# Moving the scans of two units and the last weight conversions in an RWKV-7 and feed-forward kernel

## The chip, the cores and the metric

The kernel runs on one core of a Trainium2 chip. The metric is the device time of one execution in microseconds; for each version several runs are taken and the median is compared. One further execution was recorded by the hardware profiler.

## The reference

The first half is an RWKV-7 recurrence over 768 steps for 4 batches of 8 heads of 40 features, all in float32. Its output is laid out as 3072 tokens of 320 features and goes through a feed-forward block with a hard-swish.

```python
for t in range(S):
    y[:, :, t] = np.einsum('bhd,bhde->bhe', rt, state)
    Sa = np.einsum('bhde,bhe->bhd', state, at)
    state_decay = state * wt[:, :, None, :] - np.einsum('bhd,bhe->bhde', Sa, bt)
    state = state_decay + np.einsum('bhd,bhe->bhde', vt, kt)
...
x = attn_out.transpose(0, 2, 1, 3).reshape(B * S, H * D)
h = x @ w_in                                   # 320 -> 2048
g = h * np.clip(h + 3.0, 0.0, 6.0) / 6.0
return g @ w_out                               # 2048 -> 320
```

## The kernel before

Time is cut into blocks of 64 steps. A unit is one block of two batches with all 8 heads, so 128 partitions; there are 24 units, in groups of four (NU = 4). Units 0 to 3 are group 0, and this document is about them and about the preparation of units 4 to 7.

Each unit is prepared and then stepped. Preparation (`prepare`, line 534) has named stages. W transposes the decays on TensorE (PE), copies them into a work tile `wm` and runs a scan for the running products (L555). gam takes a reciprocal, runs a second scan (L566) and copies the results into `gam` and `rgam`, two copies on VectorE (L579) and two on GpSimd (L583, L584), with `dec` (L586). A and B transpose a and b and multiply them by the gammas (L599, L607); K does so for k (L687); F, factor, E and EV make the block's triangular matrix, the scaled rows KBt, and products with them. A whole group's F is inverted by a long chain of small VectorE operations (`invert`, L733 to L767), and products of the blocks (`third_block`, L788 and L811, called X and Y for group 0) finish the inverse `tinv`.

Stepping (`step`, line 832) has the stages RT, VT (transposes), R (L868, L872), S, U and UT (products with `tinv`), C and H (masked scores, L522 and L530), rS, sn (the state's sum, L961 and L969), y (L984; L995 on VectorE, then L996 `yg` on GpSimd), and `move`, `move2`, which copy yg by eight DMAs into `xt`, the feed-forward's input. Units 0 and 1 start from a zero state. Two yg buffers are shared by `ys` and `yg`.

The feed-forward of a unit is two jobs (unit, half). A job's `expand` is five pieces of matmuls into the PSUM tile h (L1066) and, at its end, L1081 on ScalarE and L1082 on VectorE; its `contract` is four pieces (L1107). `pieces(n)` issues n pieces between other work, job after job in the order of `jobs`; when the next job may not start, nothing is issued. A job may start when the unit's `move2` was issued and enough weights are converted.

The two weight matrices come in 20 pieces of raw data that are converted on the chip: three ScalarE operations each (`power`, L384 to L386) and three on VectorE (L369, L372, L360). The generator `load_weights` yields after each of these steps, so one piece is four steps; `deal(n)` takes n steps.

All instructions are issued in a hand-made order, and each engine runs its own in that order. For group 0 this order is the text PLAN (line 1282): a line is one t, an entry such as `2rS:3` runs stage rS of unit 2 and deals three weight steps right behind the PE work of that stage, ahead of the copies out of PSUM that follow it. P and Q are units 4 and 5 with the stages W and gam only, one stage for each mention. At t = 8 `seconds()` takes over a tile that held raw weights; from t = 8 on pieces are issued behind each line, and from t = 10 on each line is followed by one turn of `by_twos`, which prepares units 4 to 7 in twos (A of 4 and 5 at t = 12; W of 6, B of 4, W of 7, B of 5 at t = 13; K at 14, factor at 15, then F). At t = 10 A of 5 and W of 7 are fetched, at t = 11 B and K of 5, at t = 12 V of 4 and 5 and R of 4. What weight steps are left when the PLAN ends follows in one go.

All DMAs wait in one queue on SyncE (SP in the profile), in order of issue; a DMA whose condition is not met holds up those behind it. Inside W of a unit the next decays for the same buffer are fetched: W of 4 issues the DMAs of W of 6.

PSUM banks: transposes take turns between the single bank "one" and the two-deep "pair"; the other products use "pair".

Of the kernel before, what the change touches and what calls it, by code (L numbers as in the profile page):

```python
# [17 lines left out]
P = 128  # L18
# [13 lines left out]
def kernel(  # L32
# [47 lines left out]
    NU = 2 * NP  # L80
# [141 lines left out]
    for i in range(3):  # L222
        t = const.tile([P, H, BL], F32, name=f"score{i}")
# [14 lines left out]
    for p in range(NP):  # L238
        t = const.tile([P, 2, NPR, SLOT], F32, name=f"state{p}")
        nc.vector.memset(t[:], 0.0)  # L240
        state.append(t)
        t = const.tile([P, 2, NPR], F32, name=f"last{p}")
# [16 lines left out]
    for i, (x, y) in enumerate([(0, DFF // 2), (0, NJ // 2)]):  # L259
        for n, z in enumerate((x, y)):  # L260
            t = win[:, :, z:z + H * SLOT] if i == 0 else \
                wout[:, z:z + 4, :].rearrange("p j m -> p (j m)")[:, 0:2 * H * SLOT].rearrange(
                    "p (n x) -> p n x", n=2)
            t = t.rearrange("p n (h e) -> p n h e", e=SLOT)
# [4 lines left out]
    for u in range(2):  # L269
        t = win2[:, u * NPR * P:(u + 1) * NPR * P]  # L270
        placed["rgam", 2 + u] = t.rearrange("p (r t) -> p r t", t=P)
    WC = 256
    PIECES = 20
    converted = [0]
# [163 lines left out]
    NK = NG * NU  # L438
# [3 lines left out]
    def fetch(name, i, engine=None):  # L442

        if i is None or i >= NK:
            return
        x, crossed = {"W": (w, 0), "A": (a, 0), "B": (b, 0), "K": (k, 0), "R": (r, 1),
                      "V": (v, 1)}[name]
        if name == "V":
            t = values[i % AHEAD]
        else:  # L450
            t = placed.get((name, i))
            if (name, i) == ("R", 1):
                t = others["K"]
            if (name, i) == ("W", NU + 1):
                t = values[NU]
            t = t if t is not None else (others if i < 2 * NU and i % 2 and name != "R" else inputs)[name]
        g, p = names[i]
        engines = engine or nc.sync
        for q in range(2):
            engine = engines[q] if isinstance(engines, tuple) else engines  # L460
            y = x[2 * p + q, :, g * BL:(g + 1) * BL, :]
            rows = slice(q * BL, (q + 1) * BL)
            if crossed:
                for s in range(2):
                    engine.dma_start(out=t[rows, 4 * s:4 * s + 4, 0:D],
                                     in_=y[s::2].rearrange("h t e -> t h e"))
            else:
                engine.dma_start(out=t[rows, :, 0:D], in_=y.rearrange("h t e -> t h e"))  # L468
        data[i][name + "N"] = t

    def following(i):

        if i < 2:
            return None
        if i < 2 * NU:

            return i + 2 if i % NU < NU - 2 or i % 2 == 0 else None
        return i + 1

    def turn_pairs(x):  # L480

        o = ps_any([P, NPR, P])
        for n in range(NPR):
            nc.tensor.transpose(out=o[:, n, :],  # L484
                                in_=x[:, 2 * n:2 * n + 2, :].rearrange("p s e -> p (s e)"),
                                identity=ident[:])
        return o
# [46 lines left out]
    def prepare(i, F):  # L534
        n, o = i % NU, data[i]
        halves = i >= 2 * NU
        def w_stage():
            wt = turn_pairs(o["WN"])
            yield PE

            wm = o["wm"] = wms[i % 2]
            wv = wm[:, 0:SCAN].rearrange("p (r m i) -> p r m i", m=2, i=HB + 1)
            x = wt[:].rearrange("p r (q m i) -> p (r q) m i", q=2, m=2)
            if i in (0, NU, NU + 1):
                nc.vector.tensor_copy(wv[:, :, 0, 1:HB + 1], x[:, :, 0, ::-1])
            else:
                nc.scalar.activation(out=wv[:, :, 0, 1:HB + 1], in_=x[:, :, 0, ::-1], func=AF.Copy)
            if i in (0, NU, NU + 1):
                nc.vector.tensor_copy(wv[:, :, 1, 1:HB + 1], x[:, :, 1, :])
            else:  # L550
                nc.scalar.activation(out=wv[:, :, 1, 1:HB + 1], in_=x[:, :, 1, :], func=AF.Copy)  # L551
            if i != NU + 1:
                fetch("W", following(i))
            prods = o["prods"] = tmp.tile([P, NB, 2, HB + 1], F32, name="prods", bufs=2)
            nc.vector.tensor_tensor_scan(  # L555
                out=prods[:].rearrange("p r m i -> p (r m i)"), data0=wm[:, 0:SCAN], data1=start[:],
                initial=0.0, op0=ALU.mult, op1=ALU.add,
            )
# [154 lines left out]
    def in_turn(stages, order):  # L713

        for name in order:
            yield from stages[name]()
            shared[0] = None
            yield DONE

    def by_stages(i, stages):  # L720


        scanned = [] if i < NU + 2 else ["W", "gam"]
        order = ["K", "factor", "F"] if i % NU < 2 else ["K", "F", "factor"]
        return in_turn(stages, scanned + ["A", "B"] + order + ["E", "EV"])
# [299 lines left out]
    HJ, NQ = NJ // 2, 4  # L1025
    SPLIT = 2
    ready = {}
    jobs = deque([(i, r) for r in range(2) for i in range(SPLIT)])
    jobs.extend((i, r) for i in range(SPLIT, NK) for r in range(2))
    sums = {}  # L1030
    narrow, spread, LATEST = [], [False], 2

    def available():
        if not jobs:
            return False
        i, r = jobs[0]
        return i in ready and converted[0] >= (PIECES // 2 if i < SPLIT and r == 0 else PIECES)

    def feed_forward():

        last = None
        while True:
            while not available():
                if last:
                    yield from contract(*last)
                    last = None
                yield None
            i, r = jobs.popleft()
            gts = []
            yield from expand(ready[i], r * NQ, gts)  # L1050
            if last:
                for n, x in enumerate(contract(*last)):
                    if n == LATEST and narrow:
                        narrow[0]()
                    yield x
            if narrow:
                narrow[0]()
            last = (i, r, gts)
# [82 lines left out]
    def pieces(n):  # L1141

        owed[0] += n * (8 / 9 if spread[0] else 1)
        while owed[0] >= 1:
            owed[0] -= 1
            if not next(stream):
                owed[0] = 0.0

    def aside(n, weight=0):

        for _ in range(n):
            if side and next(side[0], side) is side:
                side.popleft()
            due[0] += weight
            while due[0] >= 1:
                due[0] -= 1
                next(weights, None)

    def deal(n):

        for _ in range(n):
            next(weights, None)

    def run(stage, steps=0, mixed=0, deals=0):

        for at in stage:
            if at == DONE:
                return
            aside(steps, mixed)
            deal(deals)  # L1170
# [13 lines left out]
    def prepared(i):  # L1184
        nonlocal F
        if i >= NK:
            return None
        if i % NU == 0:
            F = lazy_F()
        return prepare(i, F)  # L1190
# [6 lines left out]
    def by_twos(first, steps, mixed, rate):  # L1197


        chains = [by_stages(first + i, prepared(first + i)) for i in range(NU)]  # L1200
        for t in range(TWOS):

            order = [0, 1] if t < STAGES else []
            order += [2, 3] if t > 5 else []
            if t < 2:
                order = [0, 1, 0, 1][4 * t:]
            if t == 3:
                order = [2, 0, 3, 1]
            for i in order:
                if t >= 2 or first != NU:  # L1210
                    run(chains[i], steps if t > 10 else 0, mixed)
                pieces(rate / 2)
            if t == 10:
                side.append(invert(group_F[-1], third, first == 0))
            yield
# [12 lines left out]
    chains = [in_turn(begin[i], [x[1:] for x in FIRST + BESIDE if x[0] == str(i)]) for i in range(NU)]  # L1228
# [17 lines left out]
    chains = [in_turn(stages[0], ["RT", "VT", "C", "R"]), in_turn(stages[1], ["RT", "VT", "C"])]  # L1246
# [25 lines left out]
    def block(i, j):  # L1272

        if i % NU < 2:
            if j == 0:
# [4 lines left out]


    PLAN = """X X:2 0U:4 0UT:2 1R
              0sn:2 0H:1 Y:2 P
              1U 1UT:2 0y P
              2RT:1 Y:1 Q
              1sn:1 1H:1 2VT:2 0move 0move2
              1y:2 2R Q
              2S:3 3RT:2
              1move 1move2 2U:3 2UT:1 2C:5
              3R:4 3VT  # L1290
              2rS:3 2sn:3 2H:4 3S:2
              2y:3 3U:1 3UT:10 3C:5
              3rS:1 3sn:2 3H:4 2move
              3y:1 2move2

              3move
              3move2"""
# [2 lines left out]
    chains = {str(i): in_turn(stages[i], [x[0][1:] for line in plan for x in line if x[0][0] == str(i)])  # L1300
              for i in range(NU)}
# [187 lines left out]
```

## Time and profile before

| what | value |
|---|---|
| time, median of 3 runs | 792.41 us (791.11 to 794.02) |
| profiled execution, time | 788.99 us |
| its span, first to last instruction | 787.3 us |
| granted TensorE clock, mean | 0.972 |
| PE busy | 723.7 us (92%) |
| VectorE (DVE) busy | 496.1 us (63%) |
| ScalarE (ACT) busy | 320.0 us (41%) |
| GpSimd (POOL) busy | 175.0 us (22%) |

A line of the timeline has start and duration in us, engine, source line, operation, tiles written and read, shape, count, and in brackets the idle time of that engine before it with what ended it. A line of the busy time by stretch has the stretch, its length, then busy us and instructions for each engine, the granted clock, and the DMA engines' share and rate. "x4" at SPq means four DMAs issued; the time is that of their issue, and they land later. PEld, the weight load of a matmul, runs beside PE.

### The profile page before, as it was taken

What the parts mean: (1) busy time and instruction counts of PE and PEld (TensorE: products, weight loads), DVE (VectorE), ACT (ScalarE), POOL (GpSimd) and SP (SyncE); (2) the same over time, 40 slices, a digit from 0 to 9 for tenths busy, and PEclk for the clock granted to TensorE, in tenths of its full rate; (3) what the DMA queues carried; (4) which work ended last, traced back from release to release, by engine and by line L of the source; (5) the groups of instructions that cost most, each with busy time, mean ns of one, the idle gap of its engine ahead of it and who ended that gap; (6) DMA issues with size and microseconds to landing.
All of it is one profiled execution on the core that took longest, in us unless ns stands there. A gap on an engine that the chain in (4) does not pass through costs nothing.

```text
span 787.3 us, 35307 instructions
## 1 busy us (share of the span) xinstructions
PE 723.7 (92%) x15832; PEld 614.3 (78%) x15832; DVE 496.1 (63%) x971; ACT 320.0 (41%) x664; POOL 175.0 (22%) x318
## 2 busy tenths in 40 slices
PE   4626679999999989999999999999999999999998
PEld 3625668778778878888888888888888888888886
DVE  7899995598545699345888445987435982323210
ACT  2377982214445324444334534335534224412211
POOL 6403113122222304112404212304312201000000
PEclk9856999999999999999999999999999999999999
DMA  9684554411332313223213223213221101110000
GB/s 123 115 194 129 127 153 69 75 26 29 55 68 54 66 25 58 51 43 66 46 30 64 45 48 62 50 28 64 45 55 34 33 8 30 30 30 10 14 19 17
DMA packets 174215, 45.03 MB, mean 57 GB/s; under 512 B 157424, under 2 KB 172784, under 8 KB 174064
## 3 DMA queue, kind: packets, MB, share of 16 engines
q1 hardware_dynamic: 169760, 42.03, 27.8%
q8 instruction: 125, 2.05, 1.1%
q10 hardware_dynamic: 4304, 0.74, 0.7%
q14 instruction: 26, 0.21, 0.1%
HBM read 34.08 MB, written 3.93 MB: 48 GB/s over the span
## 4 chain that ended last, share of the span: by engine, by line
PE 77%; DVE 8%; issue 5%; SPq 4%; DMA 3%; ACT 2%; POOL 1%; DVEq 0%; POOLq 0%; ACTq 0%
PE h L1066 27%; PE o L1107 24%; PE pair L522 4%; PE pair L984 3%; PE pair L494 2%; PE pair L961 2%; PE one L484 2%; SPq L468 2%; PE pair L906 2%; PE pair L868 2%; DVE prod L753 1%; DVE x L759 1%; PE pair L926 1%; PE pair L942 1%; PE pair L701 1%
## 5 line engine op out<-in xcount | busy, mean ns | idle before, releaser
L1066 PE MATMUL h<-xt,win 128*128 128x128 f32 (+1 forms) x2304 | 249.2, 282 | 2.8 <-DVE gt L1082 2.0
L1066 PEld LDWEIGHTS h<-xt,win 128*128 128x128 f32 (+1 forms) x2304 | 229.9, 191 | 19.8 <-issue 5.0
L1107 PE MATMUL o<-wout,gt 128*128 128x320 f32 x768 | 230.4, 443 | 0.0
L1107 PEld LDWEIGHTS o<-wout,gt 128*128 128x128 f32 x768 | 138.4, 190 | 50.3 <-issue 0.2
L1082 DVE SCALAR_TENSOR_TENSOR gt<-gt,h 128x512 f32<-128x512 f32 x96 | 62.0, 681 | 71.4 <-ACT gt L1081 71.3
L1081 ACT ACTIVATE gt<-h,three 128x512 f32<-128x512 f32 x96 | 62.1, 685 | 101.9 <-PE h L1066 101.4
L996 POOL TENSOR_TENSOR yg<-ys,gam 128x512 f32<-128x512 f32 x22 | 39.0, 1774 | 156.3 <-DVE ys L995 83.6
L753 DVE TENSOR_TENSOR prod<-x 128x30 f32<-128x30 f32 (+9 forms) x180 | 67.2, 373 | 8.8 <-POOL x L738 3.3
L674 POOL TENSOR_TENSOR KBt<-K,rgt 128x320 f32<-128x320 f32 x22 | 19.0, 866 | 215.6 <-ACT rgt L663 177.8
L759 DVE TENSOR_TENSOR x<-x,prod 128x30 f32<-128x30 f32 (+9 forms) x180 | 62.2, 346 | 5.5
L969 DVE TENSOR_TENSOR state<-pair,state 40x320 f32<-40x320 f32 (+1 forms) x43 | 20.9, 487 | 60.8 <-PE pair L961 34.5
L530 DVE COPY_PREDICATED score<-mask,pair 128x512 f32<-128x512 int32 x72 | 50.6, 723 | 0.5
L995 DVE TENSOR_TENSOR ys<-pair,ys 128x512 f32<-128x512 f32 x22 | 15.2, 691 | 42.9 <-PE pair L701 21.8
L566 DVE TENSOR_TENSOR_SCAN wm<-wm,start 128x528 f32<-128x528 f32 x24 | 37.5, 1562 | 0.8
L555 DVE TENSOR_TENSOR_SCAN prods<-wm,start 128x528 f32<-128x528 f32 x24 | 30.1, 1259 | 10.4 <-ACT wm L551 10.3
L846 ACT ACTIVATE RT<-pair 128x512 f32<-128x512 f32 x22 | 13.1, 596 | 52.8 <-PE pair L494 52.8
L706 ACT ACTIVATE EV<-pair 64x320 f32<-64x320 f32 x44 | 19.0, 431 | 33.7 <-PE pair L701 23.0
L821 ACT ACTIVATE tinv<-pair 32x256 f32<-32x256 f32 x48 | 17.9, 374 | 31.7 <-PE pair L811 31.1
L1125 ACT ACTIVATE ob<-o 128x320 f32<-128x320 f32 x22 | 9.6, 435 | 49.4 <-PE o L1107 29.6
L583 POOL COPY gam<-prods 128x256 f32<-128x256 f32 x24 | 22.0, 916 | 30.7 <-DVE prods L555 26.9
L872 DVE TENSOR_TENSOR RR<-pair,EV 128x320 f32<-128x320 f32 x22 | 10.7, 487 | 25.4 <-PE pair L522 25.4
L984 PE MATMUL pair<-score,KBt 64*64 64x64 f32 x1408 | 25.9, 221 | 0.5 <-issue 0.5
(272 smaller groups left out, 1066.1 us busy)
## 6 DMA issues: line engine op xcount, KB each, us to landing
V<-in_v_dram SPq DMA_DIRECT2D x96, 40.0 KB
out_dram<-ob SPq DMA_DIRECT2D x47, 80.0 KB
R<-in_r_dram SPq DMA_DIRECT2D x92, 40.0 KB
B<-in_b_dram SPq DMA_DIRECT2D x42, 80.0 KB
K<-in_k_dram SPq DMA_DIRECT2D x42, 80.0 KB
W<-in_w_dram SPq DMA_DIRECT2D x37, 80.0 KB
A<-in_a_dram SPq DMA_DIRECT2D x37, 80.0 KB
xt<-yg SPq DMA_DIRECT2D x72, 40.0 KB
```

The source lines that it names most:

```text
L522: nc.tensor.matmul(out=o[i][half(q), n, :], lhsT=lhs[half(i, D), n ^ (2 * q * swap), half(q)], rhs=rhs[half(i, D), n, half(q)], start=True ...
L530: nc.vector.copy_predicated(out=x[:].rearrange("p (i h) t -> p i h t", i=2), mask=mask8, data=o[2])
L555: nc.vector.tensor_tensor_scan(out=prods[:].rearrange("p r m i -> p (r m i)"), data0=wm[:, 0:SCAN], data1=start[:], initial=0.0, op0=ALU.m ...
L566: nc.vector.tensor_tensor_scan(out=back, data0=back, data1=start[:], initial=0.0, op0=ALU.mult, op1=ALU.add)
L753: nc.vector.tensor_tensor(out=pv, in0=_ap(x[:], (i + 1) * L + i, [[L, n], [0, i]]), in1=_ap(x[:], i * L, [[0, n], [1, i]]), op=ALU.mult,)
L759: nc.vector.tensor_tensor(out=rest, in0=rest, in1=pv, op=ALU.add)
L984: nc.tensor.matmul(out=y[q][half(s), pr, :], lhsT=o[name][half(q), h * D:h * D + SLOT], rhs=m[name][half(q), 4 * rs + 2 * s + j, :], start ...
L996: nc.gpsimd.tensor_tensor(out=yg[:], in0=m["ys"][:].rearrange("p r q t -> p r (q t)"), in1=o["G"][:], op=ALU.mult)
L1066: nc.tensor.matmul(out=hp[c][:, i, :], lhsT=lhsT, rhs=rhs, start=(begun[c] == 0), stop=(begun[c] == 3 * NQ - 1))
L1081: nc.scalar.activation(out=gt[:], in_=hp[c][:], func=AF.Relu, bias=three[:], scale=1.0)
L1082: nc.vector.scalar_tensor_tensor(out=gt[:], in0=gt[:], scalar=6.0, in1=hp[c][:], op0=ALU.min, op1=ALU.mult)
L1107: nc.tensor.matmul(out=op[:], lhsT=gts[c][:, n, :], rhs=wout[:, c * HJ + r * NQ + n, :], start=((split or r == 0) and c == 0 and n == 0), ...
```

## The change

Four things, all in the stretch of group 0 and the preparation of units 4 and 5:

- the stages W and gam of units 4 and 5 (P, Q in the PLAN) are issued at t = 11, behind H of unit 3, and at t = 12, behind y of unit 3; before, they stood between t = 1 and t = 5;
- their copies into `wm` run on ScalarE, as those of other units do;
- the first half of unit 2 becomes the third job of the feed-forward, followed by its second half and the second halves of units 0 and 1, and it may start with half of the weights converted;
- from t = 7 on fewer weight steps are dealt, and the rest at t = 12 and within `by_twos` (one step for each PE stage while its own count is under 5).

```diff
-            if i in (0, NU, NU + 1):
+            if i == 0:
                 nc.vector.tensor_copy(wv[:, :, 0, 1:HB + 1], x[:, :, 0, ::-1])
             else:
                 nc.scalar.activation(out=wv[:, :, 0, 1:HB + 1], in_=x[:, :, 0, ::-1], func=AF.Copy)
-            if i in (0, NU, NU + 1):
+            if i == 0:
                 nc.vector.tensor_copy(wv[:, :, 1, 1:HB + 1], x[:, :, 1, :])
...
-    jobs = deque([(i, r) for r in range(2) for i in range(SPLIT)])
-    jobs.extend((i, r) for i in range(SPLIT, NK) for r in range(2))
+    jobs = deque([(0, 0), (1, 0), (2, 0), (2, 1), (0, 1), (1, 1)])
+    jobs.extend((i, r) for i in range(SPLIT + 1, NK) for r in range(2))
...
-        return i in ready and converted[0] >= (PIECES // 2 if i < SPLIT and r == 0 else PIECES)
+        return i in ready and converted[0] >= (PIECES // 2 if i <= SPLIT and r == 0 else PIECES)
...
-                    run(chains[i], steps if t > 10 else 0, mixed)
+                    run(chains[i], steps if t > 10 else 0, mixed, 1 if t < 5 else 0)
...
     PLAN = """X X:2 0U:4 0UT:2 1R
-              0sn:2 0H:1 Y:2 P
-              1U 1UT:2 0y P
-              2RT:1 Y:1 Q
+              0sn:2 0H:1 Y:2
+              1U 1UT:2 0y
+              2RT:1 Y:1
               1sn:1 1H:1 2VT:2 0move 0move2
-              1y:2 2R Q
+              1y:2 2R
               2S:3 3RT:2
-              1move 1move2 2U:3 2UT:1 2C:5
-              3R:4 3VT
-              2rS:3 2sn:3 2H:4 3S:2
-              2y:3 3U:1 3UT:10 3C:5
-              3rS:1 3sn:2 3H:4 2move
-              3y:1 2move2
+              1move 1move2 2U:2 2UT:1 2C:3
+              3R:2 3VT
+              2rS:1 2sn:2 2H:2 3S:2
+              2y:2 3U:1 3UT:1 3C:4
+              3rS:1 3sn:2 3H:4 P Q 2move
+              3y:3 P Q 2move2
```

## The prediction

> **What bounds the kernel now.** The page came first: PE is busy for 723.7 of 787.3 us, and its busy tenths are low only in the first seven slices. After 200 us PE is idle 11.0 us of 587, so its work there is fixed and a delay handed to it reaches the end whole. Then busy time by stretch, cut where the change acts: from unit 1's first product to unit 3's R (74.3 to 93.6), to the end of unit 3's H (119.2), to F of unit 4 (134.0), to the B transposes of unit 6 (147.5).
>
> ```profile
> core 0: us, PE busy (x) PEld busy (x) DVE busy (x) ACT busy (x) POOL busy (x), PEclk, DMA share, GB/s
> 74.30:93.60 19.30, 12.35 (x510) 10.46 (x505) 18.57 (x38) 18.30 (x33) 4.23 (x11) 1.00 0.62 144
> 93.60:119.20 25.60, 20.93 (x553) 19.16 (x553) 23.45 (x40) 21.59 (x33) 3.05 (x6) 0.93 0.50 137
> 119.20:134.00 14.80, 14.80 (x176) 12.80 (x180) 7.68 (x13) 2.63 (x7) 2.28 (x4) 1.00 0.37 62
> 134.00:147.50 13.50, 11.62 (x298) 9.18 (x297) 8.01 (x18) 4.46 (x9) 6.25 (x10) 1.00 0.41 76
> ```
>
> Two things are to be seen. In the first stretch VectorE and ScalarE are both full, not VectorE alone. In the third PE is full while VectorE has 7.1 us free: the change moves VectorE work out of the first two and into the third.
>
> The timeline of VectorE gives the price of one early scan and gamma (unit 4):
>
> ```profile
> 75.53 0.42 DVE L545 COPY wm<-one 128x256 f32<-128x256 f32 x1
> 75.86 0.41 DVE L549 COPY wm<-one 128x256 f32<-128x256 f32 x1
> 76.31 1.26 DVE L555 TENSOR_TENSOR_SCAN prods<-wm,start 128x528 f32<-128x528 f32 x1
> ...
> 78.89 0.25 DVE L564 RECIPROCAL start<-prods 128x16 f32<-128x16 f32 x1
> 79.17 1.26 DVE L566 TENSOR_TENSOR_SCAN wm<-wm,start 128x528 f32<-128x528 f32 x1
> ```
>
> With L579 and L568 behind it, 2.0 us for the scan and 2.0 us for the gamma, so 8.1 us for both units. One weight piece (L369, L372, L360) is 0.42 + 0.69 + 0.69 = 1.8 us of VectorE, and its three L384 to L386 are 2.2 us of ScalarE.
>
> The timeline of SyncE's queue, in which every DMA waits its turn:
>
> ```profile
> 80.75 1.28 SPq L468 DMA_DIRECT2D W<-in_w_dram  x2
> ...
> 112.62 3.10 SPq L1010 DMA_DIRECT2D xt<-yg  x4
> 116.80 2.02 SPq L468 DMA_DIRECT2D B<-in_b_dram  x2
> 118.93 1.28 SPq L468 DMA_DIRECT2D K<-in_k_dram  x2
> 120.25 3.41 SPq L1015 DMA_DIRECT2D xt<-yg  x4
> 123.71 5.30 SPq L465 DMA_DIRECT2D V<-in_v_dram  x8
> ```
>
> From 120.25 on the queue has no gap until 153.9: `2move2`, V, R, A, A, W, `3move`, `3move2`, then unit 6's B at 142.51. PE and GpSimd feel that queue once each, in the timeline:
>
> ```profile
> 125.06 1.27 POOL L996 TENSOR_TENSOR yg<-ys,gam 128x512 f32<-128x512 f32 x1 [5.92 <-DMA xt<-yg]
> 133.95 1.59 PE L621 MATMUL pair<-bt,at 40*32 40x64 f32 x128
> 147.50 0.63 PE L484 MATMUL one<-ident,B 128*128 128x128 f32 x4 [1.88 <-DMA B<-in_b_dram]
> ```
>
> Unit 3's yg on GpSimd cannot start before unit 2's `2move2` has landed (two yg buffers), and PE loses 1.88 us for B.
>
> **Part 1, what leaves the early stretches.** The 8.1 us of scans and gammas go. Of the conversion, counting one step per yield, what moves behind unit 3's H is the product of piece 16 and pieces 17 to 19: 0.7 + 3 x 1.8 = 6.1 us of VectorE; pieces 18 and 19 of ScalarE's part move behind H, 17's behind unit 3's ys. The two transposes (0.66 us each on PE) and the GpSimd copies (1.4 and 1.4 us) hang on the scans and go with them; nobody waited for them.
>
> In 74.3 to 93.6 ScalarE keeps all its work, 18.30 of 19.30 us, so 8.1 us less on VectorE can give at most 1 us. The first feed-forward matmuls behind it wait for unit 0's xt anyway: its fourth DMA was issued at 92.94 and landed at 96.52 by the chain. SyncE's queue runs without a gap from 79.92 to there, and the two W DMAs above (1.28 us) leave it; with 0.3 us from the third blocks that is 1.6 us earlier.
>
> From 96.5 to 119.2 PE needs 16.8 us: 96 feed-forward matmul records at 4.66 us per 48 (the row at 174.8), 9.3 us, and 7.5 us of unit steps. It takes 22.7. Of the 5.9 us over, the waits for VectorE read 0.77 (RR), 1.24 (state), 0.86 (mask) and 0.37 us (ys); the one for gt (1.39) stays, as two pieces' ScalarE work now lies ahead of unit 3's S and of gt. I take 2.4 us. Together **-4.0 us**, bounds -1 (ScalarE holds) and -7.5 (1.6 + 5.9, PE never waits).
>
> **Part 2, the pile behind unit 3's H.** Counted from the end of H (119.19 before). VectorE's queue then holds, in order: state 0.5, the product of piece 16 and two steps of 17 (1.9), H's mask 0.7, scan 4, scan 5, the product of 17 and two steps of 18 (1.8), unit 3's ys 0.7, gamma 4, gamma 5, and only then `at` of unit 4. Scan 4 waits for its wm copies, now on ScalarE behind pieces 17 and 18: two times 2.2 us, then 0.39 + 0.38, so about 4.6 us after H. From there 2.5 + 1.8 + 0.7 + 4.0 = 9.0 us: VectorE reaches `at` at 13.6.
>
> The same operand comes by another way too. W of unit 6 is fetched right behind unit 4's transposes, and so stands on SyncE's queue ahead of `2move`, which before was issued 6.6 us ahead of H's end. Now: transposes 0.6, W 1.3, `2move` 3.1, B and K 2.6, `2move2` 3.4, landing 1.4 (123.66 to 125.06) make 12.4 us after H, where it was 5.9. Then yg 1.3, then the gamma copy of unit 4 on GpSimd, 0.40 us alone and 1.36 us beside VectorE (rows at 138.32 and 136.39): 14.1 to 15.1. I take `at` at 14.5 to 15.2, against 5.9 us before (125.08).
>
> PE comes to W of unit 6 at 8 to 9 us (6.5 before, two transposes more and the mask) and needs the PSUM bank "one", which the transposed A of unit 4 holds until `at` is done: it stands still for some 6 us. After that VectorE still has pieces 18 and 19 (the rest, 2.5), `at` 5, scans 6 and 7 (2.5), two bt and two kt (0.65 each), 8.5 us, against 6.5 us of PE work, and F of unit 4 comes at 24.0 + 0.4 + 1.1 = 25.2 to 25.5 us after H instead of 14.8. That is **+10.4 us**. Bounds: VectorE's additional work there is 6.6 (scans and gammas without copies) + 6.1 = 12.7 us; if all 7.1 us of free time took some of it, +5.6; with each GpSimd copy at 1.36, +11.9.
>
> **Part 3, what is late next.** PE reached unit 6's B at 145.62 and waited 1.88. Now it comes at 26.4 + 10.4 = 36.8 us after H. The queue of DMAs is 0.6 + 28.7 us long by the same rows, and lands 4.9 us later (142.51 to 147.37): 34.2. The wait goes: **-1.9 us** (bounds -1.9 and 0).
>
> **Part 4, the rest.** The first half of unit 2 as third job: by the running sum of pieces the plan now issues 19 until its end, 18 of which two jobs hold; matmul work is the same, and the two output sums on VectorE (L1122, 0.48 us each) only come later. Its xt lands at 5.0 + 3.6 = 8.6 us after H, its first matmul is behind the stop above: hidden, and 0 to 1 us if PE didn't stop. The four wm copies on ScalarE are counted. PE's clock: after an idle stretch of 1.5 us it was 0.55 in 162.0 to 165.8, and the next 48 matmuls took 5.29 instead of 4.66. I take **+0.5**, bounds 0 and 1.7.
>
> The Trainium skill, "TensorE: Matmul & The Clock Gate", part 1 on the clock gate, speaks against the change: a PE idle through one window of about 3.4 us is throttled to half rate until a window is busy again. Six idle us would cost one such window, 1.7 us at most by that page, and little of it while VectorE sets the pace; the sum would be up to 1.2 us higher by that rule. The trace agrees as far as it goes: its half-rate stretch followed a shorter idle.
>
> **Sum.** -4.0 + 10.4 - 1.9 + 0.5 = +5.0 us. The profiled execution has a span of 787.3 us and took 788.99, 3.4 under the median of 792.41; it becomes 792.3 and 794.0, and the median 797.4 us.
>
> **Rivals.**
> *The pile is covered* (not slower). If scans 4 and 5 run in VectorE's waits, as 7.1 us of them are there in the third stretch, and early PE waits all go: -7.5 + 5.6 - 1.9 = -3.8, up to -5 with other waits gone, 788.0 us. It decides where `at` of unit 4 ends under 9 us after H. For it: VectorE, 42.0 of 44.9 us busy before H, loses 14.2. Against: the order of its queue, with both gammas ahead of `at`.
> *Half of it*: the early stretches reach PE's bound (-7.5), the pile costs 9: about 0, 792.0 us. For it: no listed wait of PE in 96.5 to 119.2 is a DMA.
> *ScalarE holds the early stretches*: gain only 1, the pile as worked out: +8.0, 800.4 us. For it 18.30 of 19.30 us; against it the lighter deals from the second feed-forward row on.
> *The change does less than it says*: third job never ready in time. Then PE lacks the one to five pieces behind the 14th, which VectorE's stop covers: as forecast.
>
> **Chances and range.** Forecast 0.52, three quarters of it over +0.5% (4 us, about what a measurement of this kernel can tell from no change); half of it 0.20, all within; covered 0.14, nearly all faster; ScalarE 0.14, slower. So faster 0.13, within 0.34, slower 0.53. The range reaches from just above the covered case to the ScalarE case with the pile's bound: 789.5 to 802.0 us.
>
> **What would show it.** Right: H of unit 3 ends near 115; PE idle for 5 to 6 us ahead of W of unit 6 with `at` L599 as releaser; GpSimd's yg of unit 3 waiting longer than 5.92 us on a DMA; no wait for B of unit 6; the last matmul about 5 us later. Wrong: `at` of unit 4 within 9 us of H, H before 113, or VectorE idle ahead of gamma 4.

## The result and the profile after

The changed kernel takes 796.69 us (median of 5 runs, 796.2 to 797.72) against 792.1 us of the kernel before in the same comparison: 4.6 us longer, ratio 1.006, 95% interval 1.0038 to 1.0082. The forecast was 797.4 us.

The profiled execution after took 796.88 us, with a span of 795.2 us. It lies on its median, while the profiled execution of before lies 3.1 us under its own; so these two profiles differ by 7.9 us, not by 4.6. For this reason both kernels were profiled a second time (below), and four profiles are compared here. All times are in us; the rows in the middle count from the end of unit 3's H.

| mark | before | before, second | after | after, second |
|---|---|---|---|---|
| mark in sn of unit 0 | 71.61 | 72.49 | 72.45 | 72.11 |
| end of H of unit 3 | 119.19 | 122.99 | 119.25 | 118.71 |
| from there: yg of unit 3 starts | 5.9 | 5.8 | 12.0 | 12.5 |
| from there: `at` of unit 4 done | 5.9 | 5.9 | 14.5 | 14.9 |
| from there: F of unit 4 in PE | 14.8 | 14.8 | 24.4 | 25.7 |
| from there: F of unit 6 in PE | 33.3 | 34.7 | 40.8 | 42.1 |
| from there: end of the span | 668.1 | 669.0 | 675.9 | 676.3 |

The mark in sn is a product of that stage which lies 0.9 us behind the stage's first one in each of these profiles (70.69 in the first profile of before); the expectations below call it the first 0sn product.

The last row is the firm one: the part behind H is 7.5 us longer in the mean, and the two profiles of a kernel differ in it by 0.9 and 0.4. The part up to H is 2.1 us shorter in the mean, but there two profiles of the kernel before differ by 3.8.

Busy time by stretch of the first profile after, from the same 74.30 us on and cut at the same events as before (3R, end of H, F of unit 4, B of unit 6):

```profile
core 0: us, PE busy (x) PEld busy (x) DVE busy (x) ACT busy (x) POOL busy (x), PEclk, DMA share, GB/s
74.30:94.80 20.50, 16.97 (x570) 14.99 (x566) 14.21 (x26) 17.22 (x31) 1.71 (x5) 0.64 0.55 140
94.80:119.25 24.45, 20.51 (x553) 19.03 (x554) 14.87 (x26) 17.18 (x28) 2.81 (x6) 0.93 0.49 134
119.25:143.70 24.45, 17.65 (x184) 15.04 (x188) 20.97 (x36) 9.37 (x19) 4.65 (x10) 0.86 0.40 71
143.70:155.30 11.60, 11.60 (x298) 9.32 (x297) 8.02 (x18) 4.03 (x8) 6.24 (x10) 1.00 0.35 66
```

VectorE did lose its work ahead of H (42.0 us before, 29.1 now), yet the two stretches together did not get shorter with it (44.9 us before, 45.0 now; the granted clock of the first was 1.00 before and is 0.64 here). Behind H it has 21.0 us where it had 7.7, and the stretch that PE filled (14.8 of 14.8) now has 17.65 of 24.45. In the fourth stretch PE is full: the wait for B is gone.

The pile itself, in the timelines of SyncE's queue, VectorE, GpSimd and PE of the same profile:

```profile
119.87 1.27 SPq L468 DMA_DIRECT2D W<-in_w_dram  x2
121.24 3.09 SPq L1010 DMA_DIRECT2D xt<-yg  x4
124.44 1.37 SPq L468 DMA_DIRECT2D B<-in_b_dram  x2
125.90 1.27 SPq L468 DMA_DIRECT2D K<-in_k_dram  x2
127.22 2.54 SPq L1015 DMA_DIRECT2D xt<-yg  x4
```

```profile
123.45 2.40 DVE L555 TENSOR_TENSOR_SCAN prods<-wm,start 128x528 f32<-128x528 f32 x2 [0.93 <-ACT wm L551]
...
128.31 1.26 DVE L566 TENSOR_TENSOR_SCAN wm<-wm,start 128x528 f32<-128x528 f32 x1
129.62 0.27 DVE L579 TENSOR_SCALAR gam<-wm 128x256 f32<-128x256 f32 x1
...
131.62 1.14 DVE L579 TENSOR_SCALAR gam<-wm 128x256 f32<-128x256 f32 x1
...
133.12 0.66 DVE L599 TENSOR_TENSOR at<-one,gam 128x512 f32<-128x512 f32 x1
```

```profile
131.24 1.37 POOL L996 TENSOR_TENSOR yg<-ys,gam 128x512 f32<-128x512 f32 x1 [12.55 <-DMA xt<-yg]
132.56 0.46 POOL L583 COPY gam<-prods 128x256 f32<-128x256 f32 x1
```

```profile
133.84 1.12 PE L484 MATMUL one<-ident,W 128*128 128x128 f32 x4 [5.79 <-DVE at L599]
...
143.65 1.56 PE L621 MATMUL pair<-bt,at 40*32 40x64 f32 x117
...
155.31 0.60 PE L484 MATMUL one<-ident,B 128*128 128x128 f32 x4
```

VectorE is ready for `at` at 133.12, 13.9 us behind H; the gamma copy of unit 4 on GpSimd, which ends the other way, is done at 133.02. Both ways end within 0.1 us of each other, and in the second profile within 0.3 us. PE stands still for 5.79 us until that `at`, and comes to B of unit 6 without a wait.

### The profile page after: what moved, and what is told of

It reads as the page before. It is cut to its first block, busy times and chain, and to the rows that moved or that the text cites. A ratio compares the mean times of both kernels' runs of the same rounds, so it can differ in the third digit from the quotient of the medians.

```text
span 795.2 us, 35312 instructions
## 1 busy us (share of the span) xinstructions
PE 730.1 (92%) x15832; PEld 620.7 (78%) x15832; DVE 495.6 (62%) x967; ACT 321.2 (40%) x668; POOL 174.8 (22%) x318
## 4 chain that ended last, share of the span: by engine, by line
PE 73%; DVE 9%; SPq 5%; issue 5%; DMA 4%; ACT 3%; POOL 1%; POOLq 0%; DVEq 0%; ACTq 0%
PE h L1066 25%; PE o L1107 22%; PE pair L522 4%; SPq L468 3%; PE pair L984 3%; PE pair L494 2%; PE one L484 2%; PE pair L961 2%; PE pair L906 2%; DVE prod L753 2%; DVE x L759 2%; PE pair L868 1%; PE pair L926 1%; DMA xt<-yg 1%; DVE wm L566 1%
## 5 line engine op out<-in xcount | busy, mean ns | idle before, releaser
L1066 PE MATMUL h<-xt,win 128*128 128x128 f32 (+1 forms) x2304 | 249.7, 282 | 3.3 <-DVE gt L1082 3.3
L1066 PEld LDWEIGHTS h<-xt,win 128*128 128x128 f32 (+1 forms) x2304 | 230.4, 192 | 20.3 <-issue 4.2
L1081 ACT ACTIVATE gt<-h,three 128x512 f32<-128x512 f32 x96 | 62.1, 685 | 96.6 <-PE h L1066 96.2
L969 DVE TENSOR_TENSOR state<-pair,state 40x320 f32<-40x320 f32 (+1 forms) x44 | 21.4, 487 | 66.5 <-PE pair L961 40.2
L530 DVE COPY_PREDICATED score<-mask,pair 128x512 f32<-128x512 int32 x71 | 49.8, 723 | 2.4 <-PE pair L522 1.9
L995 DVE TENSOR_TENSOR ys<-pair,ys 128x512 f32<-128x512 f32 x22 | 15.2, 690 | 41.1 <-PE pair L701 21.8
L846 ACT ACTIVATE RT<-pair 128x512 f32<-128x512 f32 x21 | 12.5, 596 | 52.7 <-PE pair L494 52.7
L984 PE MATMUL pair<-score,KBt 64*64 64x64 f32 x1472 | 27.9, 225 | 1.1 <-DVE score L530 0.6
L984 PEld LDWEIGHTS pair<-score,KBt 64*64 64x64 f32 x1472 | 24.5, 138 | 3.6 <-DVE score L530 1.4
```

What stands on the lines that cost most here:

```text
L530: nc.vector.copy_predicated(out=x[:].rearrange("p (i h) t -> p i h t", i=2), mask=mask8, data=o[2])
L984: nc.tensor.matmul(out=y[q][half(s), pr, :], lhsT=o[name][half(q), h * D:h * D + SLOT], rhs=m[name][half(q), 4 * rs + 2 * s + j, :], start ...
L1066: nc.tensor.matmul(out=hp[c][:, i, :], lhsT=lhsT, rhs=rhs, start=(begun[c] == 0), stop=(begun[c] == 3 * NQ - 1))
L1081: nc.scalar.activation(out=gt[:], in_=hp[c][:], func=AF.Relu, bias=three[:], scale=1.0)
```

## The experiments

The theory: the loss is the pile behind H, built by the late scans and gammas alone, and reached by two ways, VectorE's queue and SyncE's queue through yg and GpSimd. The rivals are named in each expectation. "Tail" below is the time from the end of unit 3's H to the end of the span.

**Scans back** at their early places, their copies on VectorE again; the third job and the lighter deals stay.

```diff
-              0sn:2 0H:1 Y:2
-              1U 1UT:2 0y
-              2RT:1 Y:1
+              0sn:2 0H:1 Y:2 P
+              1U 1UT:2 0y P
+              2RT:1 Y:1 Q
...
-              1y:2 2R
+              1y:2 2R Q
...
-              3rS:1 3sn:2 3H:4 P Q 2move
-              3y:3 P Q 2move2
+              3rS:1 3sn:2 3H:4 2move
+              3y:3 2move2
```

> The changed kernel with the scans and gammas of units 4 and 5 back between t = 1 and t = 5 (copies on VectorE again); third job and lighter deals stay. Theory (the pile of scans and gammas behind H of unit 3 costs the time): the stop of PE ahead of W of unit 6 goes, the wait for B of unit 6 comes back, time 0 to 3 us under the kernel before (789 to 792). Rival (third job and late conversions cost it): still 3 us or more over the kernel before.

Measured: 791.55 us, ratio to before 1.0008 (0.9988 to 1.0028). The tail is 668.2 us, that of the kernel before. PE's stop is gone, as expected; the wait for B of unit 6 did not come back, as PE reaches B 29.0 us behind H here instead of 26.4.

**Scans only**: the kernel before with P and Q behind H and the copies on ScalarE, and nothing else of the change.

> The kernel before with only the scans and gammas moved behind H and y of unit 3; its deals and its order of jobs stay, so all conversions are done before H. Theory A (the stop has two ways to the same end: VectorE's queue, and SyncE's queue to yg to the gamma copy on GpSimd): at of unit 4 still ends 13 us or more after H, PE idle 4 us or more, time 4 to 6 us over before. Theory B (only the conversion steps among the scans make the pile too long): at ends at 9 to 10 us, PE idle under 2 us, time within 2 us of before.

Measured: 797.02 us, ratio 1.0077 (1.0061 to 1.0093). `at` of unit 4 is done 14.3 us behind H, yg of unit 3 starts at 12.0, PE stands still for 6.9 us, and the tail is 674.3 us, 5.7 longer than before. There is no conversion in the pile here, and VectorE comes to `at` early and idles for 5.31 us; PE's stop is there all the same, through the other way: theory A holds, theory B falls.

**Third job only**: the kernel before with the new order of `jobs`.

> The kernel before with only the first half of unit 2 as third job. Theory: the xt of unit 2 has landed by then, same matmul work, within 1 us of before. Rival: the third job waits for xt or its PSUM bank costs time: 2 us or more over before.

Measured: 790.52 us, ratio 1.0 (0.9981 to 1.002); tail 667.9 us. Alone it changes nothing that these runs can tell.

**Lighter deals only**: scans early and jobs as before, but the conversion stretched into the preparation of units 4 to 7.

> The kernel before with only the lighter deals (last pieces converted later); scans stay early, jobs as before. Theory: 6 us of VectorE's conversion work fall into the 7 us it has free behind H, the early stretches lose work from VectorE and ScalarE: 0 to 3 us under before, H of unit 3 one to three us earlier. Rival (the late conversions themselves hold up at and bt): 2 us or more over before.

Measured: 798.95 us, ratio 1.0102 (1.0081 to 1.0122), tail 675.0 us: the loss that the rival expected, not the theory's gain, and H did not come earlier either (see part 1 below). It differs from the first experiment in the order of `jobs` alone, and costs 7.4 us more. Busy time from 134 to 320 us, of the kernel before, of scans back, and of this one:

```profile
134.00:320.00 186.00, 177.02 (x3884) 146.87 (x3883) 131.72 (x270) 72.13 (x160) 47.70 (x83) 0.99 0.28 52
```

```profile
134.00:320.00 186.00, 178.18 (x3855) 148.31 (x3858) 134.80 (x275) 71.74 (x159) 48.66 (x84) 1.00 0.29 52
```

```profile
134.00:320.00 186.00, 172.06 (x3707) 144.47 (x3709) 132.06 (x267) 70.14 (x155) 48.32 (x84) 0.99 0.27 49
```

PE is idle 5 to 6 us more here. The late conversions did not do it by holding up `at` and bt, as the rival has it: F of unit 6 comes 33.8 us behind H, as in scans back (33.7). But up to 330 us the trace has 684 feed-forward matmuls (L1066) where it has 720 in scans back and before. With the old order the third job waits for all 20 pieces of weights, so for a while there is less feed-forward work to fill PE's waits; that this is the whole loss was not tested by itself. The third job is then the cover under which the late conversion costs nothing: neutral alone, worth 7.4 us with the lighter deals.

The next three take the two ways to `at` apart.

**2move first.**

```diff
-              3rS:1 3sn:2 3H:4 P Q 2move
+              3rS:1 3sn:2 3H:4 2move P Q
```

> The changed kernel with 2move of unit 2 issued ahead of P and Q at t = 11, so that its four DMAs no longer wait on SyncE behind the W DMAs of unit 6. Counted from the end of unit 3's H, the changed kernel had unit 3's yg at 12.0 us and the end of at of unit 4 at 14.5 us. With 2move issued before H ends, SyncE then holds W 1.3, B and K 2.6, 2move2 3.4 us, landing 1.4: yg at about 9.3, the gamma copy on GpSimd done at 12.0. Theory A (two ways, VectorE's queue to 13.6 and SyncE's to 14.1 or later): VectorE's way is left, at ends at 14.0, 0 to -0.7 us, 796.0 to 796.7 us. Rival B (VectorE's queue alone): yg earlier, at where it was, no change. Rival C (SyncE's queue alone): at ends at 12.4, -2.1 us, 794.6 us.

**No steps in the pile.**

```diff
-                    run(chains[i], steps if t > 10 else 0, mixed, 1 if t < 5 else 0)
+                    run(chains[i], steps if t > 10 else 0, mixed)
...
-              3rS:1 3sn:2 3H:4 P Q 2move
-              3y:3 P Q 2move2
+              3rS:1 3sn:2 3H P Q 2move
+              3y P Q 2move2
```

> The changed kernel without the weight steps dealt at 3H, 3y and within the first turns of by_twos; what is left of them follows in one go when the PLAN ends. VectorE's queue behind unit 3's H then holds no conversion and the copies for the scans no longer stand behind two pieces on ScalarE: its way to at of unit 4 is 0.6 + 0.9 + 2.5 (scans) + 0.7 (ys) + 4.0 (gammas) = 8.7 us, SyncE's way stays at 14.1. Theory A and rival C: at ends at 14.0 to 14.5 as before, and the three pieces in one go (5.4 us of VectorE) come ahead of bt, kt and F of unit 4: 0 to +2 us, 796.7 to 798.7. Rival B (VectorE's queue alone): at ends at 9 to 10, -2 to -4 us, 793 to 795.

**Both at once.**

> Both at once: 2move ahead of P and Q, and no weight steps in the pile. VectorE's way 8.7 us, SyncE's way 12.0. Theory A: at of unit 4 ends at 12.4 (14.5 in the changed kernel), that is 2.1 us earlier, more than the sum of the two alone (0 to 0.7 and 0); VectorE still has 21 us of work between H and F of unit 4 (20.97 of 24.45), so F comes 0.5 to 2 us earlier: 794.7 to 796.2. Rival B: as without the steps alone, at at 9 to 10. Rival C: as with 2move first alone, at at 12.4 in both.

Measured, with the changed kernel's two profiles in the first row (times in us behind the end of H, but for the last column):

| kernel | yg of unit 3 | `at` done | F of unit 4 | F of unit 6 | tail | median, ratio to before |
|---|---|---|---|---|---|---|
| changed | 12.0, 12.5 | 14.5, 14.9 | 24.4, 25.7 | 40.8, 42.1 | 675.9, 676.3 | 796.69, 1.006 (1.0038 to 1.0082) |
| 2move first | 9.3 | 14.9 | 25.0 | 41.5 | 674.3 | 796.17, 1.0066 (1.0046 to 1.0085) |
| no steps | 12.0 | 14.3 | 24.6 | 46.8 | 682.6 | 802.82, 1.0153 (1.0127 to 1.0179) |
| both | 9.1 | 11.4 | 21.4 | 45.2 | 679.1 | 799.67, 1.0113 (1.0083 to 1.0144) |

One way shortened moves `at` by nothing; both shortened move it by 3.1 us. The rows of VectorE's timeline show which way is left, first without the steps, then with both, then with 2move first:

```profile
132.64 0.69 DVE L599 TENSOR_TENSOR at<-one,gam 128x512 f32<-128x512 f32 x1 [4.60 <-POOL gam L583]
```

```profile
128.36 0.69 DVE L599 TENSOR_TENSOR at<-one,gam 128x512 f32<-128x512 f32 x1 [1.66 <-POOL gam L583]
```

```profile
133.55 0.66 DVE L599 TENSOR_TENSOR at<-one,gam 128x512 f32<-128x512 f32 x1
```

Without the steps VectorE idles for 4.60 us until GpSimd's copy; with 2move first it does not idle at all. So the theory of two ways stands, and each rival of one way falls. The times do not follow `at`, though; those of both and of no steps lie 3.5 and 4.1 us above what was expected. Taken out of the pile, the last conversion steps come in one go behind F of unit 4 (145.6 to 152.8 us on VectorE without the steps), ahead of the gammas, masks and `at` of units 6 and 7, and F of unit 6 comes 22 to 24 us behind F of unit 4 where it was 16.4. With both, PE waits 3.4 us there for one mask (L530). That work had cost less inside the pile. The tail with 2move first is 1.6 to 2.0 us shorter than in the changed kernel although no mark up to F of unit 6 comes earlier; one profile does not say why, and the median gains nothing.

**Scans in the middle**, at t = 8 and t = 10, where VectorE had come free.

```diff
-              3R:2 3VT
+              3R:2 3VT P Q
...
-              2y:2 3U:1 3UT:1 3C:4
-              3rS:1 3sn:2 3H:4 P Q 2move
-              3y:3 P Q 2move2
+              2y:2 3U:1 3UT:1 3C:4 P Q
+              3rS:1 3sn:2 3H:4 2move
+              3y:3 2move2
```

> The changed kernel with P and Q neither early nor behind unit 3's H, but at t = 8 (W) and t = 10 (gam), where VectorE is now busy 14.9 of 24.5 us, and with their wm copies on VectorE again. Theory (ScalarE, the xt transfer and the clock hold the stretch from 94.8 to 119.3, VectorE has room there): H of unit 3 ends within 1 us of the changed kernel's, at of unit 4 comes back to 6 to 8 us behind it (14.5), up to 1.9 us of wait for B of unit 6 comes back: 790.5 to 793. Rival (VectorE bounds that stretch after all, only at other places): H ends 3 to 4 us later, 794 to 796.

Measured: 796.13 us, ratio 1.0067 (1.0046 to 1.0088). H ends at 122.92, 3.7 us later than in the changed kernel, as the rival has it, but not through VectorE. PE's timeline:

```profile
96.61 1.11 PE L484 MATMUL one<-ident,V 128*128 128x128 f32 x4
97.51 1.06 PE L484 MATMUL pair<-ident,W 128*128 128x128 f32 x4
98.73 1.12 PE L484 MATMUL one<-ident,V 128*128 128x128 f32 x4 [0.16 <-ACT VT L879]
99.64 3.99 PE L1066 MATMUL h<-xt,win 128*128 128x128 f32 x24
```

The two transposes stand directly ahead of the first feed-forward matmuls, at half clock (1.1 us each where the same form takes 0.60 at full clock; the second row named V is unit 5's decays, which lie in a tile of that name). From 3R to the first feed-forward matmul 4.1 us pass, 1.1 in the changed kernel, and 0.8 us more is lost before 3R. Then `at` of unit 4 comes 11.7 us behind H, as PE reaches its transposes late: two waits (1.65 and 1.20 us) and a half-rate stretch, 126 to 133 us, lie ahead of them. Room on VectorE alone was not enough to place the scans.

**ScalarE free**: the changed kernel without the weight steps of 2U, 3R and t = 9.

```diff
-              1move 1move2 2U:2 2UT:1 2C:3
-              3R:2 3VT
-              2rS:1 2sn:2 2H:2 3S:2
+              1move 1move2 2U 2UT:1 2C:3
+              3R 3VT
+              2rS 2sn 2H 3S
```

> The changed kernel without the weight steps of 2U, 2C, 3R and of all of t = 9; they join the rest behind unit 3's H. Nothing is left out of the result. ScalarE then has no power steps ahead of U of unit 3 and of unit 3's S and the first gt. Read by the end of unit 3's H alone, counted from the first 0sn product (46.8 us in the changed kernel, 47.6 before). Theory D (ScalarE held the early stretches: PE waited 1.8 us for U and 2.7 us for gt): the wait for U goes, the one for gt falls to 0.7 to 1.4 us, H 2 to 3.5 us earlier, 43.3 to 44.8. Rival E (the transfer of unit 0's xt and TensorE's half-rate stretch at its first matmuls set the pace): the first feed-forward matmul and H where they were, 46.3 to 47.3. The whole time is 3 to 8 us longer than the changed kernel's in both, as three and a half more pieces follow behind H.

The three steps of 2C, which the expectation names, stayed where they were. Measured: H ends 44.2 us behind the mark in sn, against 46.8 and 46.6 in the changed kernel: 2.6 us earlier than in its first profile, as theory D has it. But the clock differed too. It was full from 80 to 92 us here, 0.62 and 0.72 in the changed kernel's profiles; *both*, whose order up to H is that of the changed kernel, had it full there as well, and its H ends 46.1 us behind the mark. Against that profile the gain is 1.9 us. The longest of PE's waits from unit 1's first product to the end of H (us in total, times, longest), first of the changed kernel, then of this one:

```profile
PE h L1066 <- DVE gt L1082: 2.7, 1, 2.7
PE pair L868 <- ACT U L910: 1.8, 1, 1.8
PE pair L522 <- ACT RT L846: 1.1, 1, 1.1
```

```profile
PE lent L926 <- issue: 1.7, 1, 1.7
PE h L1066 <- DVE gt L1082: 1.5, 1, 1.5
PE h L1066 <- ACT win L386: 1.2, 1, 1.2
```

The wait for U is gone and the one for gt is 1.2 us shorter, although all of the first 24 feed-forward matmuls ran at half clock here. The first row is a wait for which the profile names no releaser ("issue"), 2.3 us long in *both*; the last is new, the first feed-forward matmul waiting for its piece of weights. The steps taken away hold VectorE work as well, but in the changed kernel VectorE was not what gt waited for: ScalarE ran from 101.04 to 106.37 us without a gap, through two pieces and S, up to L1081, and VectorE idled 2.5 us for it. The whole time is 800.91 us, 1.0133 (1.0098 to 1.0168), with a tail of 681.9 us: the conversion that was taken away here comes behind H.

**Lighter t = 9**: the kernel before with the third job and a few steps of t = 9 dealt later, tried as a version better than both.

```diff
-              2rS:3 2sn:3 2H:4 3S:2
-              2y:3 3U:1 3UT:10 3C:5
-              3rS:1 3sn:2 3H:4 2move
-              3y:1 2move2
+              2rS:2 2sn:1 2H:1 3S:1
+              2y:3 3U:2 3UT:10 3C:6
+              3rS:2 3sn:2 3H:4 2move
+              3y:3 2move2
```

> The kernel before with the third job, and with five weight steps of t = 9 dealt later, at t = 10 to 12, still all ahead of the PLAN's end; scans early as before. Theory D: with fewer power steps ahead of unit 3's S and the first gt, PE's wait for gt (1.4 to 1.9 us) shrinks by about 1 us, and VectorE's waits ahead of it by up to 0.5: H 1 to 1.5 us earlier, 789 to 790. Rival (what is dealt later is waited for later, at U, UT or the second gt of unit 1): no change, 790.5 to 791.5.

Measured: 794.51 us, 1.0035 (1.0017 to 1.0053), slower than either expected. What was dealt later was waited for later, and at a higher price: H ends at 124.61, behind one wait for the mask of unit 3's C. On VectorE that mask (L530, at 121.84) stood behind five pieces' conversion, which ran there from 112.69 to 121.92.

```profile
PE pair L961 <- DVE score L530: 3.6, 1, 3.6
```

**Both kernels again**, to see what moves between two executions of one program.

> The kernel before, unchanged, profiled a second time. Its first profiled execution had a span of 787.3 us, 3 us under the median of its times. If the half-rate stretches of TensorE fall by the small shifts of an execution's start, this profile has them at other places (first: 53.2 to 73.7, 94.1 to 97.5, 162.4 to 165.8) and a span of 788 to 792 us; if they hang on the kernel alone, the same places and 787 to 788. The end of unit 3's H, counted from the first 0sn product, was 47.6 us: 47 to 50 with moved stretches, 47.4 to 47.8 without. at of unit 4 5.5 to 6.5 us behind H in both.

> The changed kernel, unchanged, profiled a second time; the first had a span of 795.2 us, H of unit 3 46.8 us behind the first 0sn product, at of unit 4 ending 14.5 and F of unit 4 coming 24.4 us behind H. What is due to the order of instructions comes again within 0.5 us (at 14 to 15, F 24 to 25, PE waiting for at 5.5 to 6.3 us); what is due to the clock may move: span 794 to 797, H 46 to 48.

Measured: medians 792.3 us for the kernel before (792.0 span in the profile) and 796.52 us for the changed one (795.0 span; ratio 1.0055, 1.003 to 1.0079). Behind H, yg and `at` came again within 0.5 us in both kernels, as in the table above. F of unit 4 came 1.3 us later in the changed kernel's second profile (25.7, expected 24 to 25), with PE at half rate for longer ahead of it. Ahead of H the kernel before lost 3.8 us against its first profile. Two stretches of the second profile at half rate, then the only one of the first profile in that part:

```profile
84.00:90.00 6.00, 6.00 (x181) 5.52 (x184) 5.83 (x12) 4.86 (x8) 2.62 (x6) 0.50 0.78 153
...
97.00:104.00 7.00, 6.89 (x60) 6.79 (x60) 6.79 (x13) 6.80 (x11) 0.67 (x2) 0.51 0.69 209
```

```profile
94.00:97.50 3.50, 3.50 (x36) 3.43 (x28) 3.22 (x7) 3.40 (x6) 0.00 (x0) 0.52 0.21 35
```

## Why the prediction was right, and where it was not

**The time** was right: 796.69 against 797.4 us, with +4.6 against +5.0. The pile and its two ways were right too. The terms, each by the means of the two profiles, were not all so close, and that their sum is so close is in part luck.

**Part 1, the early stretches** (-4.0) is the term that was mis-sized. H did not end near 115: it ended at 119.25 and 118.71, 2.1 us earlier than before in the mean of the profiles, and from the tail and the medians it is 2.2 to 2.9 us (7.5 less 5.3 or 4.6, the two comparisons of medians: 796.52 with 791.26, 796.69 with 792.1). Both of its steps were too large. The 1.6 us for an earlier xt rest on a wait that is not in the rows. The first feed-forward matmuls ran without a wait in the profile of before, ahead of the landing at 96.52 that the prediction takes for theirs, and in the first profile after they start at the same distance from the mark in sn (23.5 and 23.4 us). Ahead of them stands 3R, which waited 1.3 us for VectorE's state before and 1.8 us for ScalarE's U after. The rows, before and after:

```profile
95.14 3.99 PE L1066 MATMUL h<-xt,win 128*128 128x128 f32 x24
```

```profile
95.87 4.47 PE L1066 MATMUL h<-xt,win 128*128 128x128 f32 x24
```

The 2.4 us behind them measured 0.9. From the first feed-forward matmul to the end of H it took 23.8 to 24.1 us in the three profiles whose order up to H is that of before (before twice, third job only), and 22.7 to 23.4 in the five with the order of the changed kernel (changed twice, 2move first, no steps, both). What failed there is the list of waits that should go. The waits for RR, state and the mask did go, but ScalarE took their place: U 1.8 and 1.2 us, and gt 2.7 us in all five, where it was 1.4, 2.3 and 1.9 in the three. The text had kept gt at its old size. Before, ScalarE's part of gt (L1081) waited 1.1 us for PE and began 34.8 us behind the mark. After, PE came to it sooner, but ScalarE worked without a gap through two pieces and S and began it at 33.9; what VectorE no longer held became waiting for ScalarE. That ScalarE holds gt is shown by its gapless rows and by the run with ScalarE free (1.9 to 2.6 us earlier). How much of the missing gain is ScalarE's is not: PE's waits without a named releaser add up to between 0.5 and 5.0 us ahead of H in the five, and the wait for U was only 0.4 us in *both*, at full clock.

Nor did either half of the change bring H forward alone. Its distance from the mark in sn was 47.6, 47.9 and 50.5 us in the three, 49.2 with only the scans moved, 49.2 and 49.8 with only the lighter deals (with the old and the new order of jobs), and 46.1 to 47.0 with the two together. These are single profiles under a moving clock, but the medians less the tails say the same: ahead of H the scans alone gain 0.6 us, the lighter deals lose 0.6 and 0.0, and the two together gain 2.2 to 2.9.

In the second profile of before, ScalarE leads already with the scans early:

```profile
PE pair L868 <- ACT UT L932: 2.3, 1, 2.3
PE h L1066 <- DVE gt L1082: 2.3, 1, 2.3
```

Which of two nearly full engines is waited for thus differs between executions; the waits that the prediction read from one profile named VectorE almost alone. The rival "ScalarE holds the early stretches" had the mechanism, but took all of the gain but 1 us.

**Part 2, the pile** (+10.4) measured +10.3 in the mean: F of unit 4 came 24.4 and 25.7 us behind H (forecast 25.2 to 25.5). Up to `at` it held by its own steps. Scan 4 started 4.2 us behind H (4.6), VectorE reached `at` at 13.9 (13.6), yg started at 12.0 and 12.5 (12.4), PE stood still 5.8 and 6.1 us (some 6). Behind `at` it did not. The prediction lets VectorE's 8.5 us set F, against 6.5 us of PE work (its own 14.5 to 15.2 and 8.5 make 23.0 to 23.7, not 24.0). But PE ran without a gap from W of unit 6 to F, 9.8 and 10.7 us, for the same work that took 8.3 us in the first profile of before; the rest is its clock, below. With no conversion steps among the scans VectorE idles there for up to 1.7 us at a time, and F came no earlier than 24.0 us (scans only) and 24.6 (no steps) behind H. So PE's own work led to F, and VectorE's way with two pieces was at most as long. The size came out right with the wrong engine at its end.

**Part 3, the wait for B** (-1.9) went as forecast, in both profiles. From F of unit 4 to F of unit 6 the time shrank by 2.8 us in the mean; 1.9 of it is that wait, and most of the rest is the second profile of before, which ran there at a lower clock (0.91, against 1.00 in the first).

**Part 4** (+0.5) did not show. The whole tail is +7.5 where parts 2 to 4 make +9.0, so a gain put 1 to 2 us too large ahead of H and a loss put 1.5 us too large behind it cancelled.

**The clock.** The stop of PE was followed by a half-rate stretch in both profiles after (130.2 to 137.0 in the first), one that neither profile of before has there. From 133.84 on, W and B of unit 6 and eight feed-forward matmuls took 1.12 + 1.06 + 1.73 us, where the same forms take 0.60 + 0.60 + 1.06 a little later: 1.65 us. The rule that the prediction set beside it, from the Trainium skill, "TensorE: Matmul & The Clock Gate", Part 1, agrees with this, with its at most 1.7 us. It does not give the half-rate stretch at 162 us, which followed an idle time of only 1.54 us. How much of the 1.65 us reached the end is not shown. In the first profile after, kt on VectorE ended 0.4 to 0.5 us before PE needed the banks that it read, so at full clock VectorE would have held PE for most of it.

**Rivals.** "Covered" falls with `at` 14.5 us behind H instead of under 9. "Half of it" falls with an H only 2 to 3 us earlier. "Does less than it says" falls: the third job ran, and the lighter deals need it.

## What to carry to other kernels

When a piece of work is moved out of a busy stretch, look for the engine that is second fullest there, and count what it will make wait; here relieving only one of two nearly full engines brought 0.6 us at most. When it is moved ahead of an operand, follow every way by which that operand comes, other queues included: with two ways of nearly equal length, shortening one moved the operand by nothing. And compare profiles from a mark on, not by their spans: five profiles without late scans and with their weights in time had 667.9 to 669.0 us behind unit 3's H, though that H ended anywhere from 119.2 to 124.6.

## What the runs showed of the hardware

The clock of an unchanged program was granted differently in two executions, early in the kernel: half-rate stretches at 94 to 97.5 and 162 to 166 us in one, at 84 to 90 and 97 to 104 us among others in the next, and H ended 3.8 us later there. The Trainium skill, "TensorE: Matmul & The Clock Gate", Part 1, says that the window of the gate runs free and the effect varies by run; this case's number, 0.5% of the time, is as large as the change that was measured. In the kernel with ScalarE free, 24 matmuls ran one behind the other at half rate for 5.5 us (93.4 to 98.9), so a PE that was busy without a gap did not have its full clock back until then.

One gamma row of VectorE took 1.14 us beside GpSimd's yg, and 0.27 us two microseconds before it (the two L579 rows above): it ended 0.15 us behind yg. The Trainium skill, "SBUF — State Buffer", section "Who interferes with whom", calls the port shared by VectorE and GpSimd an exclusive lock, by which one blocks until the other is done; the row agrees. With 2move first it cost the same on another row: yg came 2.6 us earlier, fell on the gamma of unit 4 (L579 1.15 us), and VectorE reached `at` no sooner.
